# Deferring a layer norm's deviation to the q,k,v eviction, with three reorderings around it, in a fused attention and SwiGLU block

## The chip, the cores and the metric

The kernel runs on one core of one Trainium2 chip, in one launch. The metric is the device time of the run in microseconds; the median over three runs stands for a kernel, and lower is better. A profiled execution is one more run, taken with the hardware profiler; its span is the time from the first to the last instruction.

Engines are named as in the profile: PE (TensorE, matmuls and transposes; PEld its weight loads), DVE (VectorE), ACT (ScalarE), POOL (GpSimd) and SP (SyncE). All DMAs of this kernel are issued on SP's queue. `L333` means line 333 of the kernel in question; in the profile of before these are lines of the kernel before.

## What is computed

A pre-norm transformer block on one sequence of 2048 rows of 640 numbers, all in fp32. The norms have no learned scale or shift.

```python
def _layernorm(x, eps=1e-5):
    m = jnp.mean(x, axis=-1, keepdims=True)
    v = jnp.var(x, axis=-1, keepdims=True)
    return (x - m) / jnp.sqrt(v + eps)

qkv = _layernorm(x) @ wqkv              # 640 -> 3 x 640, 32 heads of 20
# each row attends to itself and to the 7 rows at distances 2, 4, ..., 14 before it
logits = einsum("bhsd,bhswd->bhsw", q, kg) * 20 ** -0.5     # masked where the row does not exist
o = einsum("bhsw,bhswd->bhsd", softmax(logits), vg)
h = x + o @ wo                          # 640 -> 640
n = _layernorm(h)
out = h + (silu(n @ w_gate) * (n @ w_up)) @ w_down          # 640 -> 1728 -> 640
```

## The kernel before

**Blocks.** The 2048 rows are four blocks of 512 (`b` 0 to 3), and each block lies on 128 partitions with four rows per partition (`j` 0 to 3). A row's 640 numbers are five chunks of 128. "Row j" below means such a tile of 128 x 640.

**Precision.** Each fp32 operand of a matmul is split into a high part (rounded by a cast on ACT) and the rest as a low part (a subtraction on DVE). A product is then three matmul passes: high by high, low by high, high by low.

**Stages of a block.**

- First norm (`LnStats` with `ln1`). For blocks 1 to 3 a row takes, on ACT, a pass that sums (L246), the sum times -1/640 (L247) and a pass that sums squares of the centred row (L248). The deviation of all four rows then takes a root on ACT (L258), and on DVE a reciprocal with one Newton step (L259 to L267). A last pass on ACT (L276) subtracts the mean and multiplies by the reciprocal deviation. For block 0, DVE does the statistics (L241, L242) and the last pass (L273), two rows at a time.
- Turning (`to_columns`). PE transposes four 128 x 128 pieces into one PSUM bank (L286), ACT copies the bank to the high part (L289), DVE writes the rest as the low part (L290). A block has five such groups, each of 512 of the 2560 columns of the four rows; so the second group needs rows 0 and 1, the third rows 1 and 2, the fourth rows 2 and 3. Banks 7, 6 and 5 take turns.
- q, k, v (`qkv`). The weights come in four groups `g` of eight heads. For each block, group and row, 15 matmuls of width 480 (L351) go into one of five banks used in turn; this is called a tile below. ACT copies the bank to a staging buffer (L357), and after every second row five DMAs write it to DRAM (L363, L371).
- Attention (`att_load`, `att_qk`, `att_exp`, `att_av`), one block and one group at a time, is done by DVE and a little ACT. K, V and q come back from DRAM (L387, L392); the products of q and K are L400, their sums L405, the softmax L412 to L426, the weighting of V L431 and L439.
- Output projection and second norm (`wo`). The attention output is turned in the same way, PE multiplies by wo (L498, two halves of 320 per row), DVE adds x (L501), and the second norm follows by the same steps as the first (ACT), its result turned again.
- Feed-forward (`ffn`, `finish`). 14 slices of the hidden size: gate and up (L538), silu and product, down (L550) into five banks. At the end DVE adds h (L597, L601) and each row goes out by one DMA (L604).

**Blocks in time.** q, k, v of all blocks come first, in the order block 0, block 1, then blocks 2 and 3 mixed; attention runs on DVE beside them. Block 0's output projection and second norm are put between the last tiles of q, k, v. Then come the four feed-forward stages, each with the next block's output projection inside it.

**What sets the order.** Every step is recorded with an engine, a cost, the ranges it reads and writes, and a priority. `Plan.order` simulates the engines with these costs and fixes the order in which each engine is given its instructions; engines then run strictly in that order. DMAs are costed with an issue time, a shared bus and a latency:

```python
LAT, DV = 3.5, (1.08, 0.05, 1.05, 0.06)
...
            if e == "SP":
                bus = max(bus, end) + nbytes / 320e3
                free[e] = max(free[e], bus - 3.0)
                end = bus + LAT
```

The steps of attention have the lowest priority (20) and yield only to a step of priority 1 that is due soon. In the built program SP's DMAs use eight completion semaphores in turn, so each DMA waits for the one eight before it.

Of the kernel before, what the change touches and what calls it, by code (L numbers as in the profile page):

```python
# [21 lines left out]
GC = D // NG  # L22
# [6 lines left out]
LAT, DV = 3.5, (1.08, 0.05, 1.05, 0.06)  # L29
PR = {'x': 6, 'wqd': 2.5, 'wqh': 0.5, 'wql': 2.5, 'qev': 1, 'kvs': 3, 'atl': 3, 'exp': 8, 'ost': 0.5, 'wod': 6, 'woh': 0.5, 'wol': 2, 'old': 1, 'fld': 3, 'fh': 2, 'fl': 8, 'ln1': 6, 't1': 2, 'wo0': 1.5, 'wo': 2}  # L30


class Plan:
# [23 lines left out]
    def order(self):  # L57
# [15 lines left out]
        while todo:  # L73
# [43 lines left out]
def dve(n):  # L117
    return DV[1] + 0.07 + 0.00104 * n * DV[0]


def tt(n):
    return 0.155 + 0.00104 * n


def act(n):
    return DV[3] + 0.09 + 0.00083 * n * DV[2]


def program(tc, x_in, wqkv_in, wo_in, ffn_in, ffl_in, const_in, out):
# [7 lines left out]
    with tc.tile_pool(name="sb", bufs=1) as sb, tc.tile_pool(  # L137
# [50 lines left out]
        EPSC, BN, MV = LN + 120, LN + 80, LN + 92  # L188
# [39 lines left out]
        class LnStats:  # L228
            def __init__(self, b, src, srcr, prio, on_dve=False):
                self.src, self.srcr, self.prio, self.on_dve = src, srcr, prio, on_dve  # L230
                base = LN + 40 * (b % 2)
                self.SUM, self.NEG, self.SS, self.STD, self.RS, self.TM, self.NB = (base + 4 * i for i in range(7))

            def one(self, j):
                src, xo = self.src, XN + 640 * j
                SUM, NEG, SS = self.SUM + j, self.NEG + j, self.SS + j
                if self.on_dve:
                    def bn():
                        st = f(BN, 12).rearrange("p (a c) -> p a c", c=6)
                        for a in range(2):  # L240
                            V.bn_stats(st[:, a, :], src(j)[:, 320 * a : 320 * a + 320])  # L241
                        V.bn_aggr(f(MV + 2 * j, 2), st)  # L242
                    P.add("DVE", 1.1, bn, r=[self.srcr(j)], w=[rf(BN, 12), rf(MV + 2 * j, 2)], prio=self.prio)
                else:
                    def s1():
                        A.activation(f(xo, 640), src(j), AF.Identity, accum_out=f(SUM, 1))  # L246
                        A.mul(f(NEG, 1), f(SUM, 1), -1.0 / D)  # L247
                        A.activation(f(xo, 640), src(j), AF.Square, bias=f(NEG, 1), accum_out=f(SS, 1))  # L248
                    P.add("ACT", 2.15, s1, r=[self.srcr(j)], w=[rf(xo, 640), rf(SUM, 1), rf(NEG, 1), rf(SS, 1)], prio=self.prio)

            def rstd(self, j, n):
                SS, STD, RS, TM, NEG, NB = (o + j for o in (self.SS, self.STD, self.RS, self.TM, self.NEG, self.NB))
                var, sc, negr = f(SS, n), 1.0 / D, [rf(NEG, n)]
                vr = rf(SS, n)
                if self.on_dve:
                    var = f(MV + 2 * j, 2 * n).rearrange("p (j c) -> p c j", c=2)[:, 1, :]
                    sc, negr, vr = 1.0, [], rf(MV + 2 * j, 2 * n)
                P.add("ACT", 0.2, lambda: A.activation(f(STD, n), var, AF.Sqrt, bias=f(EPSC, 1), scale=sc), r=[vr, rf(EPSC, 1)], w=[rf(STD, n)], prio=self.prio, table="sqrt")  # L258
                P.add("DVE", 0.15, lambda: V.tensor_scalar(f(TM, n), var, sc, EPS, op0=ALU.mult, op1=ALU.add), r=[vr], w=[rf(TM, n)], prio=self.prio)  # L259

                def newton():
                    V.reciprocal(f(RS, n), f(STD, n))
# [3 lines left out]
                    if not self.on_dve:  # L266
                        V.tensor_mul(f(NB, n), f(NEG, n), f(RS, n))  # L267
                P.add("DVE", 1.0, newton, r=negr, w=[rf(STD, n), rf(RS, n), rf(TM, n), rf(NB, n)], prio=self.prio)

            def apply(self, j):  # L270
                xo = XN + 640 * j
                if self.on_dve:
                    P.add("DVE", 0.09 + 0.00052 * 640, lambda: V.tensor_scalar(f(xo, 640), self.src(j), f(MV + 2 * j, 1), f(self.RS + j, 1), op0=ALU.subtract, op1=ALU.mult),  # L273
                          r=[self.srcr(j), rf(MV + 2 * j, 1), rf(self.RS + j, 1)], w=[rf(xo, 640)], prio=self.prio)
                else:
                    P.add("ACT", act(640), lambda: A.activation(f(xo, 640), self.src(j), AF.Identity, bias=f(self.NB + j, 1), scale=f(self.RS + j, 1)),  # L276
                          r=[self.srcr(j), rf(self.NB + j, 1), rf(self.RS + j, 1)], w=[rf(xo, 640)], prio=self.prio)
# [14 lines left out]

        def wq(g, half, k):
            return 4800 * g + 2400 * half + 480 * k
# [6 lines left out]
        def load_x(b, js=range(NJ)):  # L301
            for j in js:
                P.add("SP", 0.55, lambda j=j: Q.dma_start(f(XR + 640 * j, 640), x_in[b, :, j, :]), w=[rf(XR + 640 * j, 640)], prio=0 if b == 0 else PR["x"], nbytes=328e3)

        def ln1(b):
# [3 lines left out]
            st = LnStats(b, src, srcr, 1 if b == 0 else PR["ln1"], on_dve=b == 0)  # L309
# [397 lines left out]
```

## Time and profile before

| | us |
|---|---|
| median of 3 runs (lowest, highest) | 885.89 (885.72, 886.36) |
| profiled execution | 887.53 |
| its span | 885.6 |
| PE busy | 867.5 (98%) |
| DVE busy | 688.7 (78%) |
| ACT busy | 376.7 (43%) |

In the profile, a line of the chain gives start, length and what ran; a line of the timeline adds the instruction's shapes and, in brackets, how long the engine had been idle and what released it; a line of the groups gives the count, the busy time, the mean in ns and the idle time ahead; a line of a table of stretches gives for each engine its busy time and number of instructions (PE, PEld, DVE, ACT, POOL), then PE's granted clock as a share of full speed, the mean share of the 16 DMA engines in use, and GB/s. A line of DMA issues ends with the KB of each and the time from issue to landing.

### The profile page before, as it was taken

How to read it: one execution, taken by the hardware profiler on the slowest of the kernel's cores; microseconds unless marked ns; L12 is line 12 of the kernel's file. 1: busy time of each engine (PE TensorE's matmuls, PEld its weight loads, DVE VectorE, ACT ScalarE, POOL GpSimd, SP SyncE). 2: the span in 40 equal slices, each digit the busy share in tenths (PEclk: the TensorE clock that was granted, in tenths of full speed). 3: DMA queues.
4: the chain of work that ended last, by engine and by line, in shares of the span. 5: the costliest groups of instructions: out<-in, count | busy, mean ns of one | idle time of the engine just before them, and what ended most of it. 6: DMA issues, size and time to landing. Idle time of an engine off the chain costs nothing.

```text
span 885.6 us, 10771 instructions
## 1 busy us (share of the span) xinstructions
PE 867.5 (98%) x4136; PEld 737.8 (83%) x4136; DVE 688.7 (78%) x791; ACT 376.7 (43%) x601; POOL 2.7 (0%) x8
## 2 busy tenths in 40 slices
PE   5999999999999999999999999999999999999998
PEld 4888888898978888888888888888888888888886
DVE  8469999999999999998999999999853336333432
ACT  6757331322375243556243444653433364323321
POOL 0000000000000000000000000000000000000000
PEclk9998999999999999999999999999999999999999
DMA  9894777687656566462755563643243124322201
GB/s 301 244 264 141 193 179 186 156 257 188 166 176 193 149 206 173 142 171 89 232 154 162 184 183 104 177 162 115 90 154 121 53 90 149 120 102 90 90 30 59
DMA packets 64691, 137.17 MB, mean 155 GB/s; under 512 B 6512, under 2 KB 41968, under 8 KB 64640
## 3 DMA queue, kind: packets, MB, share of 16 engines
q1 hardware_dynamic: 64640, 136.49, 51.9%
q8 instruction: 32, 0.52, 0.3%
q14 instruction: 19, 0.16, 0.1%
HBM read 110.18 MB, written 26.29 MB: 154 GB/s over the span
## 4 chain that ended last, share of the span: by engine, by line
PE 93%; DMA 3%; DVE 1%; SPq 1%; ACT 1%; issue 0%; ACTq 0%
PE bank L538 42%; PE bank L550 21%; PE bank L351 20%; PE bank L498 8%; PE bank L286 2%; DMA fa<-in_x_dram 2%; DMA fa<-ksc 1%; DMA fa<-in_wqkv_dram 1%; DVE fa L400 0%; SPq L363 0%; SPq L392 0%; ACT shb L289 0%; PE bank L593 0%; DVE ra L333 0%; SPq L330 0%
## 5 line engine op out<-in xcount | busy, mean ns | idle before, releaser
L538 PE MATMUL bank<-shb,ra 128*128 128x512 f32 x1620 | 381.8, 390 | 1.0 <-ACT shb L289 1.0
L538 PEld LDWEIGHTS bank<-shb,ra 128*128 128x128 f32 x1620 | 302.5, 188 | 63.3 <-ACT shb L289 1.5
L550 PE MATMUL bank<-ra,acts 128*128 128x512 f32 x656 | 163.1, 392 | 0.0
L532 DVE TENSOR_TENSOR ra<-fa,ra 128x640 fp32r<-128x640 f32 (+1 forms) x164 | 131.4, 821 | 24.2 <-ACT ra L522 12.4
L550 PEld LDWEIGHTS bank<-ra,acts 128*128 128x128 f32 x656 | 121.6, 188 | 24.4
L522 ACT CAST ra<-fa 128x1280 fp32r<-128x1280 f32 (+1 forms) x56 | 68.9, 1230 | 125.0 <-PE bank L538 121.0
L351 PE MATMUL bank<-ra,sha 128*128 128x480 f32 x480 | 109.2, 386 | 0.4 <-ACT sha L289 0.3
L570 DVE TENSOR_TENSOR fa<-bank,fa 128x512 f32<-128x512 f32 x52 | 35.8, 689 | 92.5 <-PE bank L538 86.9
L351 PE MATMUL bank<-ra,shb 128*128 128x480 f32 x480 | 105.7, 379 | 0.0
L351 PEld LDWEIGHTS bank<-ra,sha 128*128 128x128 f32 x480 | 91.1, 192 | 15.0 <-ACT sha L289 1.1
L351 PEld LDWEIGHTS bank<-ra,shb 128*128 128x128 f32 x480 | 89.7, 188 | 13.3
L400 DVE TENSOR_TENSOR fa<-fa 128x2560 f32<-128x2560 f32 x32 | 90.3, 2822 | 7.6 <-DMA fa<-ksc 5.3
L431 DVE TENSOR_TENSOR fa<-fa 128x1280 f32<-128x1280 f32 x64 | 93.7, 1487 | 0.7
L439 DVE TENSOR_TENSOR fa<-fa 128x1280 f32<-128x1280 f32 (+2 forms) x96 | 89.7, 934 | 2.4
L405 DVE TENSOR_REDUCE fa<-fa 128x128 f32<-128x2560 f32 x32 | 90.1, 2816 | 0.5
L569 ACT ACTIVATE fa<-bank 128x512 f32<-128x512 f32 x52 | 31.2, 599 | 117.0 <-PE bank L538 116.9
L357 ACT COPY st<-bank 128x480 f32<-128x480 f32 x64 | 35.7, 557 | 100.8 <-PE bank L351 84.3
L498 PE MATMUL bank<-ra 128*128 128x320 f32 x480 | 74.8, 309 | 0.0
L498 PEld LDWEIGHTS bank<-ra 128*128 128x128 f32 x480 | 72.6, 188 | 2.2
L524 ACT CAST ra<-fa 128x640 fp32r<-128x640 f32 x56 | 40.8, 731 | 53.0 <-PE bank L550 52.7
L286 PE MATMUL bank<-fa 128*128 128x128 f32 x240 | 35.7, 286 | 13.1 <-DVE fa L273 8.9
L550 PE MATMUL bank<-acts,ra 128*128 128x512 f32 x164 | 46.4, 391 | 0.0
(64 smaller groups left out, 470.3 us busy)
## 6 DMA issues: line engine op xcount, KB each, us to landing
fa<-in_ffn_dram SPq DMA_DIRECT2D x52, 960.0 KB, 4.7
fa<-ksc SPq DMA_DIRECT2D x32, 440.0 KB, 5.9
fa<-vsc SPq DMA_DIRECT2D x32, 440.0 KB, 5.8
fa<-in_x_dram SPq DMA_DIRECT2D x32, 320.0 KB, 3.3
ksc<-st SPq DMA_DIRECT2D x64, 80.0 KB, 3.7
vsc<-st SPq DMA_DIRECT2D x64, 80.0 KB, 3.0
qsc<-st SPq DMA_DIRECT2D x32, 160.0 KB, 3.0
fa<-qsc SPq DMA_DIRECT2D x16, 320.0 KB, 6.2
```

The source lines that it names most:

```text
L286: T.transpose(banks[bk][:, 128 * q : 128 * q + 128], src(4 * u + q), ident)
L351: T.matmul(banks[bk][:, 0:480], t()[:, o : o + 128], r_(wq(g, w, c), 480), start=p == 0 and c == 0, stop=p == 2 and c == NC - 1)
L400: P.add("DVE", dve(2560), lambda: V.tensor_tensor(f(PROD, 2560).rearrange("p (j w c) -> p j w c", j=2, w=W), window(ko, 2 * jp), f(qo + 32 ...
L405: P.add("DVE", dve(2560), lambda: V.tensor_reduce(f(lo + 128 * jp, 128), f(PROD, 2560).rearrange("p (n d) -> p n d", d=DH), axis=AX.X, op= ...
L431: V.tensor_tensor(f(PROD + 1280 * jj, 1280).rearrange("p (w h d) -> p w h d", w=W, d=DH), f(vo + 160 * j, 1280).rearrange("p (w h d) -> p ...
L439: V.tensor_add(dst(v), v[:, :, 0:m, :], v[:, :, m : 2 * m, :])
L498: T.matmul(banks[bk][:, 0:320], r_(o, 128), r_(m, 320), start=p == 0 and c == 0, stop=p == 2 and c == NC - 1)
L522: P.add("ACT", act(n), lambda: A.copy(r_(gu, n), f(raw, n)), r=[rf(raw, n)], w=[rr(gu, n)], prio=PR["fh"])
L524: P.add("ACT", act(640), lambda: A.copy(r_(dn[0], 640), f(raw + n, 640)), r=[rf(raw + n, 640)], w=[rr(dn[0], 640)], prio=PR["fh"])
L532: P.add(eng, c, lambda o=o: E.tensor_sub(ra[p0:, lo + o : lo + o + 640], fa[p0:, raw + o : raw + o + 640], ra[p0:, hi + o : hi + o + 640]. ...
L538: T.matmul(banks[bk], r_(gu + 1280 * w + wid * c + col, 128), x2(a, c), start=p == 0 and c == 0, stop=p == 2 and c == NC - 1)
L550: T.matmul(banks[k], l, m, start=first and p == 0, stop=last and p == len(passes) - 1)
```

## The change

- **First norm.** It only centres. For rows 0 to 2 of block 0, DVE takes the statistics and subtracts the mean (`one_dve`); for all other rows ACT sums, centres, and takes the squares of the centred row in a step of its own (priority one lower), written over the loaded x. The reciprocal deviations get a place of their own per block (`RS1`), and the q, k, v eviction is an `Identity` activation that multiplies by them. In block 0 they are worked out row by row, elsewhere for four rows at once.
- **Opening.** x rows and the weight loads of the first group alternate one by one; each matmul of block 0's first group is a step of its own that waits for its own chunk; the first weight casts get priority 1.2.
- **Second norm of block 0.** Its deviation is worked out for rows 0 to 2 when row 2 is there, and for row 3 alone. The last q, k, v tile reads the high part of x from a copy (`XH`).
- **Last output row.** Its sum is made in two halves of 256 and written with two DMAs, the second half first.
- **The planner's costs.** DMA latency 1.8 instead of 3.5 us, bus 350 instead of 320 GB/s, issue 0.45 instead of 0.55, larger costs for the small stores, and new costs for ACT and DVE. Priorities `wqh` and `woh` (the other weight casts) go from 0.5 to 3.

The core of the diff, shortened:

```diff
-LAT, DV = 3.5, (1.08, 0.05, 1.05, 0.06)
-PR = {..., 'wqh': 0.5, ..., 'woh': 0.5, ...}
+LAT, RATE = 1.8, 350e3
+PR = {..., 'wqh': 3, ..., 'woh': 3, ...}
...
-                bus = max(bus, end) + nbytes / 320e3
+                bus = max(bus, end) + nbytes / RATE
...
                 def s1():
                     A.activation(f(xo, 640), src(j), AF.Identity, accum_out=f(SUM, 1))
                     A.mul(f(NEG, 1), f(SUM, 1), -1.0 / D)
+                    if self.center:
+                        A.activation(f(xo, 640), src(j), AF.Identity, bias=f(NEG, 1))
+                    else:
                         A.activation(f(xo, 640), src(j), AF.Square, bias=f(NEG, 1), accum_out=f(SS, 1))
...
+                if self.center:
+                    P.add("ACT", 1.0, lambda: A.activation(src(j), f(xo, 640), AF.Square, accum_out=f(SS, 1)),
+                          r=[rf(xo, 640)], w=[self.srcr(j), rf(SS, 1)], prio=self.prio + 1)
...
+            def one_dve(self, j):
...
+                    V.bn_aggr(f(MV + 2 * j, 2), st)
+                    V.tensor_scalar(f(xo, 640), self.src(j), f(MV + 2 * j, 1), None, op0=ALU.subtract)
...
 def ln1(b):
-            if b == 0:
-                for j in range(NJ):
-                    st.one(j)
-                    if j % 2:
-                        st.rstd(j - 1, 2)
-                        st.apply(j - 1)
-                        st.apply(j)
-            else:
-                for j in range(NJ):
-                    st.one(j)
-                st.rstd(0, 4)
-                for j in range(NJ):
-                    st.apply(j)
+            for j in range(NJ):
+                (st.one_dve if b == 0 and j < 3 else st.one)(j)
+            st.prio = 2
+            for j in range(NJ) if b == 0 else ():
+                st.rstd(j, 1)
+            if b:
+                st.rstd(0, NJ)
...
 def qkv(b, g):
+                moved = (b, g, j) == (NB - 1, NG - 1, NJ - 1)
+                if moved:
+                    P.add("ACT", act(640), lambda j=j: A.copy(r_(XH, 640), ...), ..., prio=3)
...
-                for ps in ((0,), (1,), (2,)) if b == g == 0 else ((0, 1, 2),):
+                whole = tuple((p, c) for p in range(3) for c in range(NC))
+                for ps in [(x,) for x in whole] if b == g == 0 else [whole]:
...
-                P.add("ACT", act(480), lambda bk=bk, so=so: A.copy(stage_t()[:, so : so + 480], banks[bk][:, 0:480]), r=[pb(bk)], ...)
+                P.add("ACT", act(480), lambda bk=bk, so=so, j=j: A.activation(stage_t()[:, so : so + 480], banks[bk][:, 0:480], AF.Identity, scale=f(RS1 + 4 * b + j, 1)),
+                      r=[pb(bk), rf(RS1 + 4 * b + j, 1)], ...)
...
 def wo(b, prio, bks):
                 stats.one(j)
-            return stats
+                if j == NJ - 1 or (j == 2 and prio < PR["wo"]):
+                    lo, n = (0, NJ) if prio >= PR["wo"] else ((0, 3), (3, 1))[j - 2]
+                    stats.rstd(lo, n)
+                    for q in range(lo, lo + n):
+                        stats.apply(q)
...
 def finish(b):
+                cuts = (0, 256, 512) if b == NB - 1 and j == NJ - 1 else (0, 512)
+                pieces = list(zip(cuts, cuts[1:]))[::-1]
+                for o, e in pieces:
...
-        load_x(0, (0, 1))
+        load_x(0, (0,))
         P.add("SP", ..., Q.dma_start(f(MASK, 160), const_in), ...)
-        load_wqkv(0, (0, 1, 2))
+        load_wqkv(0, (0, 1))
+        load_x(0, (1,))
+        load_wqkv(0, (2, 3))
         load_x(0, (2,))
-        load_wqkv(0, (3, 4))
+        load_wqkv(0, (4,))
         load_x(0, (3,))
```

More of the change, by code (lines that the diff above doesn't have):

```diff
@@ L251, in rstd, with s1 @@
-            def rstd(self, j, n):
[L252 to L259, printed above, removed]
+                def s1():
+                    A.activation(f(xo, 640), src(j), AF.Identity, accum_out=f(SUM, 1))
+                    A.mul(f(NEG, 1), f(SUM, 1), -1.0 / D)
+                    if self.center:
+                        A.activation(f(xo, 640), src(j), AF.Identity, bias=f(NEG, 1))
+                    else:
+                        A.activation(f(xo, 640), src(j), AF.Square, bias=f(NEG, 1), accum_out=f(SS, 1))
@@ new lines, in qkv, with mm @@
+                if moved:
+                    P.add("ACT", act(640), lambda j=j: A.copy(r_(XH, 640), t()[:, 640 * j : 640 * j + 640].bitcast(F32)), r=[(nm, 640 * j, 640 * j + 640)], w=[rr(XH, 640)], prio=3)
+                def mm(ps, j=j, bk=bk, moved=moved):
+                    for p, c in ps:
+                        a, w = passes[p]
+                        o = 2560 * a + 640 * j + 128 * c
+                        l = r_(XH + 128 * c, 128) if moved and a == 0 else t()[:, o : o + 128]
+                        T.matmul(banks[bk][:, 0:480], l, r_(wq(g, w, c), 480),
+                                 start=p == 0 and c == 0, stop=p == 2 and c == NC - 1)
```

129 lines of the change are left out of this document (61 added, 68 removed).

## Prediction, made before the changed kernel ran

> **What bounds the kernel now.** First the head of the page: who is busy, and through whom the chain runs that ends last.
>
> ```profile
> span 885.6 us, 10771 instructions
> PE 867.5 (98%) x4136; PEld 737.8 (83%) x4136; DVE 688.7 (78%) x791; ACT 376.7 (43%) x601; POOL 2.7 (0%) x8
> PE 93%; DMA 3%; DVE 1%; SPq 1%; ACT 1%; issue 0%; ACTq 0%
> ```
>
> PE sets the end. The change leaves its matmuls and transposes as they are (the same counts line by line), so it can only give or take time in which PE waits or runs slowly. Where that is, the chain in order of time tells (start, length, what; pieces left out between them):
>
> ```profile
> 16.91 16.92 PE bank L351 x76
> ...
> 40.96 9.32 DMA fa<-in_x_dram
> 50.30 6.84 DMA fa<-in_x_dram
> 57.16 6.55 DMA fa<-ksc
> 63.73 2.83 DVE fa L400
> 67.54 0.93 ACT fa L276
> 68.51 2.82 PE bank L286 x12
> 71.33 4.55 PE bank L351 x15
> 96.21 1.31 PE bank L286 x12
> 97.52 25.94 PE bank L351 x120
> 258.73 14.15 PE bank L538 x60
> 878.40 3.47 PE bank L550 x15
> ```
>
> Undisturbed, a q,k,v matmul takes 25.94 / 120 = 0.216 us (a tile of 15: 3.24) and a transpose 1.31 / 12 = 0.109. PE is off this pace in four places: before 16.91; around 68.5; just ahead of 258.73; and after 881.9, where only the last output is left. Then what PE waited for, and its clock (column PEclk, the third from the right):
>
> ```profile
> PE bank L286 <- DVE fa L273: 8.9, 2, 8.5
> PE bank L286 <- ACT fa L276: 3.3, 1, 3.3
> 67.00:68.00 1.00, 0.00 (x0) 0.00 (x0) 0.93 (x4) 0.46 (x1) 0.00 (x0) 0.62 0.35 88
> 68.00:74.00 6.00, 5.49 (x20) 5.00 (x21) 5.93 (x8) 4.80 (x8) 0.00 (x0) 0.50 0.87 262
> 39.00:58.00 19.00, 19.00 (x94) 16.56 (x93) 14.71 (x11) 10.45 (x26) 0.00 (x0) 1.00 1.01 269
> fa<-ksc SPq DMA_DIRECT2D x32, 440.0 KB, 5.9
> ```
>
> The wait before 68.51 is 3.3 us, and PE then ran on half its clock: 12 transposes in 2.82 instead of 1.31, 15 matmuls in 4.55 instead of 3.24. The place costs 3.3 + 1.5 + 1.3 = 6.1 us. Its cause is the chain above: attention's second K load was issued at 57.16, behind the x loads, and landed at 63.7; DVE stood at the product of L400 in front of block 2's deviation (four Newton steps), and the norm's last step (L276) and PE's transposes waited for that.
>
> **The change, part by part.** *Opening.* Rows used:
>
> ```profile
> 3.73 0.89 DVE L241 BATCH_NORM_STATS2 fa<-fa 128x6 f32<-128x320 f32 x2 [1.66 <-DMA fa<-in_x_dram]
> 7.85 1.14 DVE L273 TENSOR_SCALAR fa<-fa 128x640 f32<-128x640 f32 x2
> 4.97 0.43 SPq L303 DMA_DIRECT2D fa<-in_x_dram  x1
> fa<-in_x_dram SPq DMA_DIRECT2D x1, 320.0 KB, 6.1
> 4.02 5.63 DMA fa<-in_wqkv_dram
> 13.42 0.16 DVE L263 TENSOR_TENSOR fa<-fa 128x2 f32<-128x2 f32 x1
> 13.62 0.16 DVE L264 SCALAR_TENSOR_TENSOR fa<-fa 128x2 f32<-128x2 f32 x1
> 14.95 0.75 ACT L246 ACTIVATE fa<-fa 128x640 f32<-128x640 f32 x1 [0.24 <-DMA fa<-in_x_dram]
> 16.04 0.83 ACT L248 ACTIVATE fa<-fa 128x640 f32<-128x640 f32 x1
> L289 ACT CAST sha<-bank 128x512 fp32r<-128x512 f32 x10 | 5.4, 589 | 0.0
> L290 DVE TENSOR_TENSOR sha<-bank,sha 128x512 fp32r<-128x512 f32 x10 | 6.4, 684 | 0.9 <-ACT sha L289 0.8
> L333 DVE TENSOR_TENSOR ra<-fa,ra 128x480 fp32r<-128x480 f32 x20 | 12.0, 652 | 2.7 <-ACT ra L331 2.7
> ```
>
> I measure by an equivalent start: the moment from which PE, at full pace, would have done the same. Before, 15 tiles and 40 transposes are done when PE stops at 68.51 - 3.32 = 65.19: 65.19 - 225 x 0.216 - 40 x 0.109 = 12.2. After: the first eight loads are the same bytes in another order, so x2 lands where the eighth landed, 4.02 + 5.63 = 9.65, and x3 at 4.97 + 6.1 = 11.1. By bytes between 3.73 and 9.65, x1 lands near 6.8. One row on DVE is statistics 0.89, their aggregate about 0.25 and a subtraction 1.14 / 2: 1.7. DVE has two weight residuals (L333, 0.65 each) first and ends x1 at 9.1, then a residual copy (0.68), then x2 at 11.6. ACT casts the fifth weight, copies x's second group, and centres x3 from 11.5 for 16.04 + 0.83 - 14.95 = 1.9: 13.4. The last two groups of transposes (8 x 0.109) end at 14.3, with 11 matmuls done among them: 14.3 - 20 x 0.109 - 11 x 0.216 = 9.7 as equivalent start. I add 0.7 for a clock still low (PE is sparsely busy until 11.5, and the next two copies of 0.59 come behind x3's square) and 0.3 for waits on single copies: 10.7, a **gain of 1.5**. Ends: 2.2 with neither, 0 if PE stays slow for 4 us more. The deviations move behind this: 4 rows x 5 steps x 0.2 (13.62 - 13.42) are 4 us on DVE instead of two groups; they delay the last two low weight parts: on DVE 11.6 + copy 0.7 + 10 steps 2.0 + copy 0.7 + weight 0.65 + two copies 1.4 + 10 steps 2.0 + two weights 1.3 = 20.4. PE asks for the last at its 41st matmul, 10.7 + 2.2 + 40 x 0.216 = 21.5: hidden, with 1 us to spare. The eviction's multiplication waits for a deviation now; a bank is asked for again only five tiles (13 us of PE) later, so 64 such evictions cost nothing. Should that cover go, PE waits for Newton steps, as before.
>
> *The middle.* Transposes of blocks 1 to 3 need centring alone, so Newton steps no longer stand before them. But the program asks for them earlier: block 2's first group after tile 11 instead of 15, the second and third after tile 12, the fourth after 14. From the equivalent start, tile 11 ends at 10.7 + 11 x 3.24 + 40 x 0.109 = 50.7, and tile 14 at 50.7 + 12 x 0.109 + 3 x 3.24 = 61.7. Block 1 first: its first centring stands on ACT behind six weight casts, 13.4 + three copies 1.8 + square 1.0 + two roots 0.6 + casts 3.5 + 1.9 = 22.2, and PE asks for it two matmuls into tile 4, at 10.7 + 2.2 + 47 x 0.216 = 23.1: hidden if those weights land in time. SP waits, at each DMA, for the one eight before it, so loads queue. x2's first row is issued at 40.9 as before (the row 40.96), but one K half and Q went out before the stores; 1.35 MB of K and V plus its own 0.33 at 269 GB/s (the row 39:58) is 6.2 us: lands 46 to 47.5, centred by 49.5. Needed at 50.7: hidden. The next two rows are issued as soon as the V halves land (45, 46) and follow on ACT at 1.9 each with an eviction and a square between, to about 51.5 and 54; needed at 54.4 and 54.7: hidden, by 0.7 for the second.
>
> The second K is the hard point. In the new order DVE does the product with it **before** the residual copy of block 2's first group, for which PE's fourth group waits (same bank). From the first K's second half (39.1) to this one 5.2 MB go out (five K or V halves of 440 KB, four x rows, one of wo, one of q, two sets of stores): 19.3 us, so 58.4. Product 2.83, copy 0.68: 61.9, against 61.7. I take 1.5 us for all waits of this stretch together (0 to 3.3), none over 2 us, so no clock drop: **gain 6.1 - 1.5 = 4.6**.
>
> *Second norm of block 0.* Rows:
>
> ```profile
> 241.97 0.88 DVE L501 TENSOR_TENSOR h<-bank,fa 128x320 f32<-128x320 f32 x2
> 249.30 1.74 ACT L276 ACTIVATE fa<-h,fa 128x640 f32<-128x640 f32 x2 [0.86 <-DVE fa L267]
> 254.18 1.47 PE L286 MATMUL bank<-fa 128*128 128x128 f32 x12
> ```
>
> Before, all 20 transposes come after the last q,k,v tile, 254.2 to 258.73: 4.55 us for 2.18 of work, 2.35 lost to copies. After, rows 0 to 2 are normalised at once and row 3 alone, and tiles stand between the groups: the last two groups go ahead of the last tile, whose 3.24 us cover two copies (1.2). Before, the way from row 3's addition to the end of the last L276 was 241.97 to at least 249.30 + 4 x 0.87 = 252.8, 11 us with four rows in it; row 3 alone needs about three L276 less, 8 to 9, where the new order leaves four tiles, 13 us. An extra table load and a copy of 640 on ACT sit in the same slack. **Gain 1.9**, ends 0 and 2.35 (0.4 for the last residual copies, which the third pass of the first FFN tile asks for).
>
> *Last output row.*
>
> ```profile
> 879.32 3.62 SPq L604 DMA_DIRECT2D out_dram<-h  x4
> 881.89 0.69 DVE L597 TENSOR_TENSOR h<-bank,h 128x512 f32<-128x512 f32 x1 [0.44 <-PE bank L550]
> out_dram<-h SPq DMA_DIRECT2D x1, 320.0 KB, 2.2
> ```
>
> One addition of 0.69 and one DMA of 320 KB become two additions, about 0.13 longer together, and two DMAs, the first some 0.3 earlier, the last only 128 KB. The data thus start 0.3 earlier. **Gain 0.3**, ends -0.2 (a second issue on SP) and 0.6.
>
> Sum: 1.5 + 4.6 + 1.9 + 0.3 = 8.3. The profiled execution took 887.53, 1.93 beyond its span, and becomes 879.2; the median of the runs is 885.89, 1.64 below it, and becomes **877.6**.
>
> **The clock, row and rule.** PE stopped at 65.19; with a mean of 0.62 between 67 and 68 the clock halved at 67.24, 2.05 us into the wait, and held until 74. So I price any new wait over 2 us at 2.8 more. [...]
>
> **The rivals.** *The wait moves with its clock drop*: K lands near 61 instead of 58.4, PE waits 61 + 3.5 - 61.7 = 2.8, and 2.8 more by the clock: the middle gains 0.5 instead of 4.6, **881.7**. For it: DMA share 1.01 in this stretch, and my slack is below 1 us. Chance 0.15.
>
> *DVE gives it back*: attention on DVE sets when block 0's output projection can run, so what PE gains before is lost there; only norm and tail stay, 885.89 - 2.2 = **883.7**. For it: DVE is 78% busy over all. Against: the new order asks three tiles later, and DVE's own longest wait (K at 63.7) shrinks too. 0.06.
>
> *The order does not deliver*: no gain in the opening (tile 14 then ends at 63.2), and K at 65, little later than the 63.7 of before: product and copy to 68.5, PE waits 5.3 + 2.8 = 8.1 instead of 6.1; with 2.2 from norm and tail **885.7**. 0.08.
>
> *Slower*: the second K, at its new place in front of the copy, lands later than before, because SP waits for stores that lie behind the x loads. From 67.0 on PE loses 8.8 + 2.8, 1.8 us more than all gains return; at 67.5 it is 9.3 + 2.8 = 12.1 against 6.1, less 3.7 of gains: **888.2**. Against: the same traffic landed it at 63.7. 0.11.
>
> **How the numbers follow.** 0.60 is left for the forecast, whose own range is 874.7 (all upper ends: 11.2) to 880. 0.2% (1.8 us) is about what a measurement can tell: 884.1 and 887.7. Faster: 0.60 + 0.14 + 0.05 = 0.79; same: 0.08 and the 0.02 left of the second and third case, 0.10; slower 0.11. The range goes from 874.7 to 884.8 and leaves out the last two rivals.
>
> **What would show it.** Right: PE's equivalent start near 10.7; no idle over 2 us and PEclk 1.00 between 17 and 254; the first FFN matmul within 0.5 us of the last q,k,v tile; 2.7 us or less from PE's end to the span's end. Wrong: PEclk below 1 after 20 us, a PE wait on DVE's residual copy or ACT's centring near 23, 50, 62 or 72 us (block 3), or any new wait of over 1 us in the FFN, where I expect none.

## The result and the profile after

| | us |
|---|---|
| before, median of 15 runs (lowest, highest) | 885.72 (884.41, 887.92) |
| after, median of 15 runs (lowest, highest) | 889.66 (886.12, 895.22) |
| after / before | 1.0043, 95% interval 1.0026 to 1.0061 |
| profiled execution of after, its span | 895.22, 893.4 |

The change makes the kernel 0.43% slower; 877.6 was predicted. The runs of after also spread wider (9.1 us from lowest to highest against 3.5), and the profiled execution is the slowest of the 15: what it shows lost is 5.6 us more than a typical run loses, and its single waits are to be read with that in mind. Part of the spread is PE's clock: the runs with a mean granted clock of 1.000 took 886.7 to 889.2, those with 0.996 or 0.997 took 891.0 to 895.2.

The head of the page of after:

```profile
span 893.4 us, 10812 instructions
PE 869.9 (97%) x4136; PEld 738.4 (83%) x4136; DVE 687.0 (77%) x801; ACT 388.4 (43%) x613; POOL 2.7 (0%) x8
```

PE still sets the end. What it waited for in after (line, releaser, then us in total, times, longest):

```profile
PE bank L298 <- DVE sha L302: 4.2, 1, 4.2
PE bank L298 <- ACT fa L247: 4.0, 2, 3.2
PE bank L362 <- ACT sha L301: 2.4, 2, 1.8
PE bank L298 <- DMA fa<-osc: 2.2, 2, 1.6
PE bank L298 <- DVE ra L302: 0.8, 1, 0.8
PE bank L567 <- DVE acts L597: 0.7, 1, 0.7
```

(`sha`, `shb` and `ra` hold the split operands of matmuls, `osc` is the attention output in DRAM, `acts` the products of silu.) The one wait of 3.3 us of before has become 8.2 us in three: centring (L247) for block 2's transposes, and the residual copy (L302) that holds the fourth group's bank. The waits for the output projection's input are new too: near 205 us for a residual (0.8, output `ra`), near 210 for the attention output (1.6), and 0.6 once more in the FFN. The chain of after shows what is behind the first of them:

```profile
36.77 8.14 DMA fa<-ksc
44.92 3.95 DMA fa<-vsc
...
54.49 6.22 DMA fa<-in_wo_dram
60.73 8.32 DMA fa<-ksc
...
71.82 0.69 DVE sha L302
...
72.56 1.11 PE bank L298 x4
73.67 8.64 PE bank L362 x30
...
262.04 3.25 PE bank L362 x15
265.29 13.60 PE bank L555 x60
```

The second half of the second K is issued at 60.73 and lands at 69.05, where the prediction had 58.4. Its product (2.82) and the copy (0.69) follow, PE starts again at 72.56, and for the next 9.8 us it does four transposes and 30 matmuls that take 6.9 at full pace. At the end of the extract the first FFN matmul follows the last q,k,v tile without a gap. The stretches around the wait (PE's busy time is the first column after the length, its clock the third from the right):

```profile
40.00:57.00 17.00, 13.83 (x71) 11.79 (x70) 10.58 (x12) 8.96 (x21) 0.00 (x0) 1.00 1.02 272
67.00:72.00 5.00, 1.37 (x7) 0.87 (x5) 2.93 (x2) 3.06 (x6) 0.00 (x0) 0.94 0.98 217
72.00:77.00 5.00, 4.45 (x13) 3.89 (x14) 4.90 (x9) 1.86 (x4) 0.00 (x0) 0.50 0.98 307
```

Why the data are late shows in SP's timeline (start, length, what was issued). First before, then after:

```profile
23.69 0.53 SPq L330 DMA_DIRECT2D fa<-in_wqkv_dram  x1
26.91 2.86 SPq L456 DMA_DIRECT2D fa<-in_wo_dram  x4
37.65 1.42 SPq L392 DMA_DIRECT2D fa<-ksc  x2
```

```profile
30.43 0.54 SPq L338 DMA_DIRECT2D fa<-in_wqkv_dram  x1
34.83 1.88 SPq L469 DMA_DIRECT2D fa<-in_wo_dram  x4
36.77 0.51 SPq L405 DMA_DIRECT2D fa<-ksc  x1
42.82 0.49 SPq L405 DMA_DIRECT2D fa<-ksc  x1
46.41 0.52 SPq L317 DMA_DIRECT2D fa<-in_x_dram  x1
```

The last weight load of q,k,v goes out 6.7 us later, four loads of wo (1.3 MB) stand right ahead of the first K instead of 10 us earlier, and the first K's second half waits at SP for the eighth DMA before it, the fourth of those wo loads: 42.8 instead of 38.4. Block 2's first x row goes out at 46.41, not 40.96, and ACT begins on it at 54.03.

### The profile page after: what moved, and what is told of

Read it like the earlier page. It is cut to its first block, busy times and chain, and to the rows that moved or that the text cites. A ratio compares the mean times of both kernels' runs of the same rounds, so it can differ in the third digit from the quotient of the medians.

```text
span 893.4 us, 10812 instructions
## 1 busy us (share of the span) xinstructions
PE 869.9 (97%) x4136; PEld 738.4 (83%) x4136; DVE 687.0 (77%) x801; ACT 388.4 (43%) x613; POOL 2.7 (0%) x8
## 4 chain that ended last, share of the span: by engine, by line
PE 91%; DMA 5%; DVE 2%; ACT 1%; SPq 1%; issue 1%; DVEq 0%; ACTq 0%
PE bank L555 40%; PE bank L362 20%; PE bank L567 20%; PE bank L511 8%; PE bank L298 3%; DMA fa<-ksc 2%; DMA fa<-osc 1%; DMA fa<-in_wo_dram 1%; DVE fa L413 1%; DMA fa<-in_wqkv_dram 1%; DMA fa<-vsc 0%; ACT ra L339 0%; DVE fa L418 0%; SPq L376 0%; DVE ra L549 0%
## 5 line engine op out<-in xcount | busy, mean ns | idle before, releaser
L362 PE MATMUL bank<-ra,sha 128*128 128x480 f32 x480 | 112.4, 392 | 2.4 <-ACT sha L301 2.4
L362 PEld LDWEIGHTS bank<-ra,shb 128*128 128x128 f32 x470 | 87.6, 188 | 12.8
L369 ACT ACTIVATE st<-bank,fa 128x480 f32<-128x480 f32 x64 | 42.0, 660 | 94.7 <-PE bank L362 78.0
L298 PEld LDWEIGHTS bank<-fa 128*128 128x128 f32 x240 | 30.5, 147 | 24.6 <-DVE fa L264 5.4
```

What stands on the lines that cost most here:

```text
L298: T.transpose(banks[bk][:, 128 * q : 128 * q + 128], src(4 * u + q), ident)
L362: T.matmul(banks[bk][:, 0:480], l, r_(wq(g, w, c), 480), start=p == 0 and c == 0, stop=p == 2 and c == NC - 1)
L369: P.add("ACT", act(480), lambda bk=bk, so=so, j=j: A.activation(stage_t()[:, so : so + 480], banks[bk][:, 0:480], AF.Identity, scale=f(RS1 ...
```

## The experiments

Runs of one group were timed beside the kernel before on one chip: before took 885.78 beside e1 to e5, 885.56 beside e6 to e9, 884.40 beside e10 to e13. So medians of different groups compare through the ratios. Four kernels move single steps within one engine's list and leave every other list as after has it; the lists are then merged again by their dependencies. `low` is a weight chunk's low part (group, chunk), `newton` a deviation of block 0 (row), `turn` a group of four transposes, `rest` its residual copy (6 to 10 block 1, 11 to 15 block 2, 16 to 20 block 3, 21 to 25 block 0's output projection), `qk` a product with K (block, group, half), `mm` a tile (block, group, row).

```diff
+        seq = {e: [n for n in P.order() if P.ops[n][0] == e] for e in ("PE", "ACT", "DVE", "POOL", "SP")}
+        move([...], before)      # within one engine's list
```

| run | kernel | median | ratio to before, 95% interval |
|---|---|---|---|
| e1 | after, low parts first on DVE | 889.26 | 1.0044 (1.0027 to 1.0060) |
| e2 | after, one residual copy first on DVE | 890.27 | 1.0051 (1.0032 to 1.0069) |
| e4 | after, PE's transposes of blocks 2 and 3 later | 888.53 | 1.0032 (1.0017 to 1.0047) |
| e5 | all of these | 888.53 | 1.0038 (1.0023 to 1.0054) |
| e6 | after, two DMA figures of the planner | 883.40 | 0.9967 (0.9955 to 0.9979) |
| e7 | after, all planner figures of before | 899.69 | 1.0150 (1.0136 to 1.0163) |
| e8 | before, planner figures of after | 891.74 | 1.0070 (1.0058 to 1.0082) |
| e9 | after, filled opening | 886.73 | 1.0013 (0.9999 to 1.0027) |
| e10 | before, second norm in two steps | 885.33 | 1.0002 (0.9991 to 1.0014) |
| e11 | before, deferral alone | 891.38 | 1.0068 (1.0052 to 1.0084) |
| e12 | before, figures as in e6 | 883.10 | 0.9984 (0.9975 to 0.9992) |
| e13 | e6, filled opening | 881.51 | 0.9961 (0.9948 to 0.9975) |

### One wait at a time: e1, e2, e4, e5

**e1.**

```diff
+        move([("low", 0, 3), ("low", 0, 4)], ("rest", 4))
+        move([("newton", 2), ("newton", 3)], ("low", 2, 0))
```

> The kernel after with only DVE's order changed in the first 25 us: the low parts of the first group's last two weight chunks and those of the second group stand ahead of block 0's last deviations (Newton steps of rows 2 and 3). Theory A, late data: those Newton steps held weight slots that SP wanted to load into (SP waited 4.5 us in one piece), the DMA engines ran at 150 GB/s from 16 to 24 us, and so everything behind came late. Then SP's longest wait for the residuals of L341 falls from 4.5 to under 2 us, x's first row of block 2 and the second half of the second K land 3 to 4 us earlier (54.0 and 69.1 in the profile of after), and the waits for centring (3.2 and 0.9 us) go; the wait for the residual of block 2's first group stays at about 4, because PE now asks earlier too; median about 886.5. Rival B or C (DVE's or PE's own order at block 2 is the cause, or landings are set by the stores and the eight outstanding DMAs): K still lands at 68 to 69, time within 1 us of the 889.7 of after.

SP's waits for the residuals of L341 before 40 us, first of after, then of e1, and PE's waits in e1:

```profile
SPq L338 <- DVE ra L341: 7.4, 9, 4.5
```

```profile
SPq L338 <- DVE ra L341: 4.0, 9, 1.5
```

```profile
PE bank L298 <- ACT fa L247: 2.7, 2, 1.9
PE bank L298 <- DVE sha L302: 2.7, 1, 2.7
```

The mechanism is there: SP's longest wait falls from 4.5 to 1.5 us, ACT begins block 2's first row at 51.6 instead of 54.0, the product with the second K starts at 65.2 instead of 69.1. The time does not follow: 889.26. From 20 us on SP ran into the next thing in its list, the stores of the first tiles, which wait for evictions near 24 us. Theory A explains part of the lateness and none of the median.

**e2.**

```diff
+        move([("rest", 11)], ("qk", 0, 1, 0))
```

> The kernel after with one instruction moved on DVE: the residual copy of block 2's first group ahead of the product with the second K. Theory B, DVE's order: the wait of 4.2 us goes, and the half clock behind it, 4 to 7 us of the profiled execution; the next residuals, which stand behind the sums and the weighting of V, then hold the fifth group and block 3's groups for some 2 us; median about 886.5. Theory C (PE's transposes of block 2 stand too early in its queue, whatever DVE does first): the wait moves to the next groups with its clock drop, median 888 to 890. Theory A alone (only the landing of the data counts): as C.

The wait of 4.2 us is gone, as theory B says. In its place PE waits 1.6 us at 79 for the next residual, the waits for centring (2.3) and osc stay, and 890.27 is what theory C expected.

**e4.**

```diff
+        move([("turn", 11)], ("mm", 0, 3, 1)); move([("turn", 12)], ("mm", 0, 3, 2))
+        move([("turn", 13)], ("mm", 0, 3, 3)); move([("turn", 14)], ("mm", 1, 0, 0))
+        move([("turn", 15)], ("mm", 1, 0, 1))
+        move([("turn", 16), ("turn", 17), ("turn", 18)], ("mm", 1, 1, 0))
```

> The kernel after with only PE's order changed: block 2's five groups of transposes each one or two tiles later, block 3's first three behind the fourth tile of block 1 instead of the first. Their columns are wanted only from the 33rd tile on. Theory C: with the data as late as before (K at about 69) the waits of 3.2, 0.9 and 4.2 us and the half clock fall to about 2 us together; worked out from the median of before: 885.7 + 0.6 (opening) - 6.1 (its stall in the middle) - 2.35 + 2.35 (second norm, and the waits for the attention output near 205) + 1.3 (FFN) + 2 = 883.5. Theories A and B, with DVE and DMA as the bound: the waits come back a few tiles later, median 887 or more.

The stretches of e4, and its longest wait:

```profile
40.00:87.00 47.00, 46.83 (x236) 40.32 (x236) 35.93 (x39) 37.12 (x83) 0.00 (x0) 1.00 0.85 226
87.00:186.00 99.00, 94.36 (x433) 81.66 (x432) 97.07 (x85) 26.73 (x44) 0.00 (x0) 0.97 0.70 178
```

```profile
PE bank L298 <- DVE shb L302: 4.6, 1, 4.6
```

Between 40 and 87 us PE now waits 0.17 us in all, with full clock. But at 121 us it stops for 4.6 us: block 3's transposes need a residual copy that stands on DVE behind attention's next products, and DVE (97.07 us busy of 99) gets there no earlier.

**e5** adds the output projection's transposes to all three:

```diff
+        move([("turn", 24)], ("mm", 2, 3, 0)); move([("turn", 25)], ("mm", 2, 3, 2))
```

> The three edits of the other runs together, and the last two groups of block 0's output projection one and two tiles later (they waited 0.8 and 1.6 us near 205 and 210 for a residual and for the attention output). Theory C with A and B as contributions: no wait of PE over 1 us between 20 and 265 us, clock full; by the same sum 885.7 + 0.6 - 6.1 - 2.35 + 1.3 = 879.1. Rival, DVE gives it back: what PE gains before 190 it waits for at the attention output near 205, 883 to 885.

Missed by 9 us: the same 4.6 us near 122, then small waits near 205 to 250. In the four kernels a wait went or shrank when its cause was taken away; the first FFN matmul came at about 260 us in e1, e4 and e5 alike, and the median stayed at 888.5 to 890.3. So the loss has no single place: the list as a whole is out of step.

### Why the list is out of step: e6, e7, e8, e12

The planner of the kernel gives each step a time while it makes the list, and the step that ends an attention unit (its store of the output, L445 or L458) can be set against the chip. These are the planner's own numbers, no measurement; beside them the issue of that store in the trace:

| kernel | plan: first unit, end of all | chip: first unit, median |
|---|---|---|
| before | 86.4, 891.0 | 88.0, 885.7 |
| after | 79.8, 881.1 | 95.1, 889.7 |
| e8 | 82.1, 886.2 | 87.1, 891.7 |
| e6 | 85.7, 887.0 | 84.9, 883.4 |
| e7 | 96.9, 903.2 | 98.5, 899.7 |
| e10 | 86.4, 890.5 | 84.5, 885.3 |
| e11 | 97.1, 897.7 | 96.6, 891.4 |
| e12 | 91.3, 891.1 | 85.7, 883.1 |

With the change's DMA figures (after, e8) the chip is 5 to 15 us behind the plan at the first unit and 5.5 to 8.6 us above it at the end; with the other figures it is within 6 us and 3.5 to 8 us below. The change's latency of 1.8 us and 350 GB/s stand against median landings of 3 to 8 us, kind by kind, between 30 and 75 us and 270 to 275 GB/s in the full stretches (272 in the row 40:57). The opening is another matter: there after moved 352 GB/s (5.4 to 17.3 us), so 350 fits the first microseconds and not the middle.

One profile tells the time of the first unit only roughly: e10 has the plan of before up to there, and its unit ended at 84.5 against 88.0. The 15 us of after also come from the slowest of its runs; e9, which has the lists of after and only fills PE's waits in the opening, ended that unit at 88.4, still 8.6 behind its plan.

**e6.**

```diff
-LAT, RATE = 1.8, 350e3
+LAT, RATE = 3.5, 280e3
```

> The kernel after with two figures of the planner changed: DMA latency 3.5 us instead of 1.8 and bus 280 GB/s instead of 350 (the timeline shows 270 to 275 where the DMA engines are full). Theory P: in the order of after the plan ends block 0's attention units at 79.8, 105.9, 134.1, 160.8 us, the chip at 95.1, 121.6, 149.1, 176.0, while the plan of before (86.4, 113.4, 142.8, 170.5) is met within 2 us (88.0, 115.6, 143.5, 171.8); so after places what PE needs from DVE and from DMAs 10 to 15 us too early in PE's queue. With these figures the plan says 85.7, 111.5, 140.3, 166.9: the waits of PE between 40 and 215 us fall from 11 to below 5 us and the median to 883 to 885. Rival E (the edits themselves, the deferral above all, cost the time): the median stays at 888 to 890.

```profile
40.00:186.00 146.00, 146.00 (x707) 127.18 (x706) 136.79 (x126) 68.28 (x131) 0.00 (x0) 1.00 0.77 210
```

```profile
252.14 14.18 PE L555 MATMUL bank<-shb,ra 128*128 128x512 f32 x60 [0.35 <-ACT shb L301]
```

Right, at 883.40. With one line changed and every other edit of the change in place, PE does not wait once from 40 to 186 us, the second K's product starts at 61.6 without waiting for the DMA, and the first FFN matmul comes at 252.14 (before: 258.73, after: 265.29).

**e7** takes all figures and the two priorities back (gathered and shortened here).

```diff
-LAT, RATE = 1.8, 350e3
+LAT, RATE = 3.5, 320e3
-'wqh': 3, ... 'woh': 3, nbytes=130e3, nbytes=250e3, issue 0.45, dve(n) = 0.155 + 0.00104 * n, act(n) = 0.155 + 0.00087 * n
+'wqh': 0.5, ... 'woh': 0.5, nbytes=82e3, nbytes=164e3, issue 0.55, dve(n) = 0.12 + 0.00112 * n, act(n) = 0.15 + 0.00087 * n
```

> The kernel after with all planner figures and the two priorities of before: the edits to the norms, the opening and the last row alone. Theory P: no slower than before, 883 to 886, if the order that comes out does not put attention late (its plan ends the first unit at 96.9, later than before). Rival E: 888 to 890, as after.

Missed: 899.69, the slowest of all. Here the plan and the chip agree (first unit 96.9 and 98.5): the list itself is bad, with attention 10 us later than before, and the second norms of later blocks wait for it (6.9 us at one in the FFN). The planner takes the next ready step by priority and looks no further, so another set of steps can send it down a worse path that its own total of 903.2 shows.

**e8** is before with `LAT, RATE = 1.8, 350e3`, the priorities and the step costs of after, and nothing else.

> The kernel before with the planner figures and the two priorities of after and none of the other edits. Theory P: its plan ends the first attention units at 82.1, 107.5, 135.6, 162.8; the chip will end them 5 to 10 us later, PE gets new waits, and the median rises to 887 to 890. Rival E: within 1 us of before, 885.7.

```profile
PE bank L285 <- ACT fa L275: 4.6, 2, 3.2
PE bank L285 <- DMA fa<-osc: 2.6, 3, 1.8
```

891.74: without any edit to the norms, the opening or the last row, the new figures alone cost 6.2 us, and leave the same marks as in after, PE stopped at block 2's transposes and at the output projection's input.

**e12** is e8 with `LAT, RATE = 3.5, 280e3`.

> The kernel before with the planner figures and priorities of after, but DMA latency 3.5 us and bus 280 GB/s, and none of the other edits: what the figures that made the edits faster than before are worth without them. Theory P with edits that are worth something: its plan ends at 891.1, with such figures the chip came out 3.6 below, so about 887; the edits then bring 3 to 4 of the difference to the 883.4 with them. Rival, the gain came from the figures alone: 883 to 884.

883.10. In ratios to their own runs of before, 0.9984 here and 0.9967 in e6: the figures bring about 0.16%, the edits about as much again, and that second part is no larger than what the two intervals leave open. The rival was nearer than the forecast.

### The parts alone: e10, e11

**e10.**

```diff
+                if prio < PR["wo"] and j >= 2:
+                    stats.rstd(0 if j == 2 else 3, 3 if j == 2 else 1)
...
+                    P.add("ACT", act(640), lambda j=j: A.copy(r_(XH, 640), ...), ...)
```

> The kernel before with one part of the change: block 0's second norm in two steps (rows 0 to 2, row 3) and the copy of x's high part that the last q,k,v tile reads. The order up to 200 us is that of before. If the gap of 2.35 us ahead of the first FFN matmul was worth what the prediction took for it: no gap of over 0.5 us there, median 883.9. Rival, the FFN gives it back (DVE is 95% busy there and the planner's end falls by only 0.5, from 891.0 to 890.5): the gap goes, and 885.0 to 885.7 remains.

PE's waits from 230 us on:

```profile
PE bank L357 <- ACT ra L350: 0.9, 1, 0.9
PE bank L548 <- ACT shb L289: 0.8, 1, 0.8
PE bank L286 <- DVE fa L588: 0.4, 1, 0.4
```

The gap of 2.35 us is gone. 0.9 of it comes back as a wait for the copy of x (L350), and the last two, 1.2 us together, stand near 413, at the next block's second norm, where before had none. Ratio 1.0002: the rival was right.

**e11.**

```diff
-                for j in range(NJ):
-                    st.apply(j)          # blocks 1 to 3: centring only, deviation to RS1
...
+  A.activation(..., AF.Identity, scale=f(RS1 + 4 * b + j, 1)) if b else A.copy(...)
```

> The kernel before with the deferral alone, in blocks 1 to 3 (block 0's norm, the opening, the second norm, the last row and the planner as before). If the deferral by itself is worth the stall at block 2 that it was to remove: 880 to 882. Theory P (the order that the planner makes of it decides): its plan ends block 0's attention units at 97.1, 123.4, 152.5, 179.7 against 86.4, 113.4, 142.8, 170.5 and the whole at 897.7 against 891.0; with the old figures the chip came out 3.5 to 5.4 below the plan, so 892.3 to 894.2.

891.38, a little below the forecast of theory P. PE's waits from 265 us on:

```profile
PE bank L300 <- ACT fa L290: 4.7, 2, 4.1
```

The first FFN matmul came at 253.8, 4.9 us earlier than before, and all of it and more was lost behind it: attention ran 8 to 9 us late from its first unit (96.6), and PE waited for the second norms of later blocks, 4.7 us near 578; the mean clock from 500 to 700 us is 0.97, which makes some 12 us of half clock (0.03 x 200 / 0.5, an estimate, the mean being given to 0.01).

### The opening: e9, e13

```diff
+        for t, n in (("w1", 8), ("w2", 5), ("w3", 6), ("w4", 5)):   # e9: 8, 4 and 1
+            P.add("PE", 0.0, lambda: [T.matmul(banks[4][:, 0:128], f(PROD, 128), f(PROD + 128, 128), ...) for _ in range(n)], ...)
```

> The kernel after with 13 small products of zeros into an unused bank, which keep PE busy where it waits before 12 us (8 ahead of the first transposes, 4 behind them, 1 behind the second group). In the profile of after the matmuls ran at half pace until 17.0 us, in that of before until about 13; the equivalent start was 12.8 against 12.2. Theory W: a trickle of work does not raise the clock, a filled one does: with the filling the pace is full from about 9 us on and the equivalent start is 10.5 to 11.3. As the waits behind it hang on data and on DVE, the median falls by 0 to 1 us only, to about 889. Rival: data hold the opening, the equivalent start stays at 12.5 to 13.

PE's timeline of before, of after and of e9 (a matmul of q,k,v takes 0.216 us at full pace, a transpose 0.109; a line is some 0.2 longer than these add up to, as with 1.31 for ten transposes):

```profile
14.68 1.31 PE L286 MATMUL bank<-fa 128*128 128x128 f32 x10 [0.38 <-DVE fa L273]
```

```profile
5.44 1.11 PE L298 MATMUL bank<-fa 128*128 128x128 f32 x4 [5.44 <-DVE fa L264]
13.65 2.35 PE L362 MATMUL bank<-ra,sha 128*128 128x480 f32 x5
17.07 8.05 PE L362 MATMUL bank<-ra,sha 128*128 128x480 f32 x36
...
56.01 0.66 PE L298 MATMUL bank<-fa 128*128 128x128 f32 x4 [3.17 <-ACT fa L247]
```

```profile
5.47 0.66 PE L303 MATMUL bank<-fa 128*128 128x128 f32 x4
11.48 0.91 PE L367 MATMUL bank<-ra,sha 128*128 128x480 f32 x2 [0.74 <-ACT sha L306]
15.93 8.04 PE L367 MATMUL bank<-ra,sha 128*128 128x480 f32 x36
```

In before the transposes at 14.68 run at full pace; in after the five matmuls at 13.65 still take 0.47 each. Filled from 2.12 us on (e9), the transposes at 5.47 run at full pace, but behind the remaining waits (1.1 and 0.7 us) half pace is back: the four transposes at 12.19 take 1.05 and the five matmuls at 12.90 take 2.35, and the mean clock from 8.50 to 17.32 is 0.81. The equivalent start is 16.17 - 11 x 0.216 - 20 x 0.109 = 11.6 against 12.8: a partial filling. The median gains 2.9 us, more than the 0 to 1 forecast. In its profile the three waits of the middle are 2.2, 0.9 and 1.9 us at full clock, against 3.2, 0.9 and 4.2 with half clock in the slowest run of after; whether the other 1.7 come from there is not settled.

> The kernel after with latency 3.5 us and 280 GB/s in the planner, and 24 small products of zeros that fill PE's waits before 12 us. With the figures alone the equivalent start was 12.3 and PE had no wait over 1 us from 20 to 500 us, so here an earlier opening should arrive at the end: equivalent start 10.3 to 11.3, median 881.8 to 882.4. Rival, what is gained early is waited for later at DVE or a DMA: 883.0 to 883.4.

```profile
56.61 1.04 PE L302 MATMUL bank<-fa 128*128 128x128 f32 x8
250.06 14.14 PE L559 MATMUL bank<-shb,ra 128*128 128x512 f32 x60 [0.35 <-ACT shb L305]
```

With the waits filled all the way, 13 tiles and 40 transposes are done at 56.61: equivalent start 56.61 - 195 x 0.216 - 4.36 = 10.1, 2.1 us ahead of e6, which stands at the same point at 58.67. The trace keeps this to the end: the first FFN matmul comes at 250.06 against 252.14, the span is 879.7 against 881.8. The median, 881.51, lies just under the range and 1.9 below that of e6, but e6 ran on another chip, and the ratios (0.9961 and 0.9967) differ by less than their intervals; so the 2 us are seen in one trace of each and not shown by the medians. The kernel is 0.39% (0.25 to 0.52) faster than before, the lowest ratio here, and by the ratios 0.8% faster than after.

## Why the prediction was wrong, point by point

The sum was to move the span by -8.3 us; the profiled spans moved by +7.8. Of the 16.1 between them the points below name 15; 1 us of small waits is not assigned. The medians moved by +3.9, so some 4 us of this belong to the profiled run and not to a typical one.

- **Opening: +1.5 forecast, -0.6 measured.** PE stopped at 52.84 (56.01 - 3.17) with 11 tiles and 40 transposes done: equivalent start 52.84 - 165 x 0.216 - 4.36 = 12.8, against 12.2 before and 10.7 forecast. The data came about as worked out (x1 centred at 9.9, x2 at 12.1, x3 at 13.8; forecast 9.1, 11.6, 13.4). Mis-sized was the allowance of 0.7 for a low clock: the trickle of single matmuls left PE at half pace until 17. The end given for that case was 0, and it fell below even that. e13 bears out the other terms: with the waits filled it started at 10.1, where the sum without the clock's 0.7 gives 9.7 + 0.3 = 10.0.
- **Middle: +4.6 forecast, about -5 measured** (8.2 of waits and 2.8 of half pace against 6.1). The step that failed is the count "From the first K's second half (39.1) to this one 5.2 MB go out ...: 19.3 us, so 58.4", in its start and in its bytes. 39.1 is the moment at which the issue of that half ended in before; like "x2's first row is issued at 40.9 as before", it was carried over from the order of before. In after that issue ended at 43.3 (42.82 + 0.49), 4.2 us later, and from there to the landing at 69.05 are 25.7 us instead of 19.3. The stretch of after:

```profile
42.80:69.05 26.25, 21.53 (x105) 17.98 (x103) 14.62 (x14) 18.81 (x44) 0.00 (x0) 1.00 0.97 254
```

254 GB/s for 26.25 us are 6.7 MB, 1.5 more than counted: the count took the bus as free at its start, while the first half of that K, issued at 36.77, landed only at 44.9. In before, too, that stretch had taken 24.6 us (39.1 to 63.7). The centring of block 2's first row, forecast for 49.5 and called hidden, ended at 55.95. I had worked out that the deviations delay the low weight parts and hidden that behind PE alone; the weight slots they free are also what SP loads into, and SP's list stands still behind them (7.4 us of such waits in after before 40 us, 4.0 in before).
- **"DVE gives it back", 0.06.** In the form given, PE's gain lost at the output projection, it did not happen in after, since there was no gain. But e4 and e5 show a kin of it as soon as the middle is mended: a copy that stands behind attention's products on DVE holds PE for 4.6 us, earlier than this rival had it. In e6 DVE is nearly as busy (136.8 us of 146) and PE does not wait, so the order decides, not DVE's load alone.
- **The slower rival, 0.11,** named the mechanism at 67: a K that lands late because of what stands before it on SP. It was right in kind, at 69.05, and its price (8.8 + 2.8 from 67.0 on) counts the one wait; PE's own lateness of 4 us by then, through centring that the prediction called hidden, made that wait shorter and the sum about the same.
- **Second norm: +1.9 forecast, 2.35 measured at its place**, no gap ahead of the first FFN matmul. It went again: 2.35 us of new waits (osc and residual) around 205 and 210, and 1.26 in the FFN, where 624.4 us lie between the first matmul and PE's end against 623.1. "Any new wait of over 1 us in the FFN, where I expect none" was nearly right in size (0.6 and 0.7) and wrong as a sum. e10 shows that the part alone is worth nothing.
- **Last row: +0.3 forecast, 0.0 measured.** From PE's end to the span's end 3.73 us before and 3.74 after: the issue of the last DMA ends 0.24 later after PE's end, and what follows it is as much shorter. The sign named for this part, 2.7 us or less, did not follow from the sum: 3.73 - 0.3 is 3.4.
- **The clock's price.** Forecast: 2.8 more for any wait over 2 us. Measured: 3.17 us in after cost nothing more (clock 1.00 throughout), 2.30 in e2 and 2.71 in e1 came with half clock for 3.4 us, 4.18 in after and 4.64 in e4 for 6.8, 4.62 in e5 for 3.4 again. So the length of a wait alone, 2 us or another, did not set the price here; the last section has the rows.
- **What no step had: the planner.** The prediction counted each edit against the trace and took the list as given. e6, e8 and e12 show that the two DMA figures, which carry no instruction, moved the time by 6 to 8 us (1.0043 to 0.9967 and 1.0070 to 0.9984 of before), more than the other edits bring under the same figures (0.9984 to 0.9967). Under the figures of before those edits even cost 1.5% (e7), again through the list that came out. The list of after was there to be read, and its distances (x issued, K issued, transposes wanted) were read against the times of before. Open is which of the two figures matters more, whether values between these two pairs would do as well, and why e12 lies so far below its plan.

## What to carry to other kernels

Where an order is made from modelled costs, set a few of the model's own times beside the trace before any edit is priced: here one line of DMA figures moved the time by 0.8%, and all the changes to the computation, under the better figures, by about 0.2%. A wait that is mended by itself in a list that is out of step comes back at the next place where two engines meet; e1, e2, e4 and e5 took such waits away and gained 1.1 us at most. And a moment taken from the old trace holds for the new order only if everything ahead of it on the same queue is still ahead of it.

## What the runs showed of the hardware

- The half clock that came with a wait of PE lasted 3.41 us in e1, e2 and e5, and 6.8 in before, after and e4. Half-microsecond stretches (PE's busy time, then its clock) of e2 and of after, at the fall and at the rise:

```profile
55.50:56.00 0.50, 0.29 (x2) 0.62 1.13 359
59.00:59.50 0.50, 0.50 (x4) 0.97 0.75 110
```

```profile
71.00:71.50 0.50, 0.00 (x0) 0.90 1.04 247
78.00:78.50 0.50, 0.50 (x4) 0.78 0.59 165
```

With 0.50 in between, e2's half clock lasts from 55.62 to 59.03, 3.41 us, and that of after from 71.40 to 78.22, 6.82. By the same reading it was 6.83 in before and in e4, 3.41 in e1 and e5. The length of the wait does not tell which: 2.30 us (e2), 2.71 (e1) and 4.62 (e5) go with 3.41, and 3.32 (before), 4.18 (after) and 4.64 (e4) with the longer ones. The wait of 3.17 us in after, from 52.84 to 56.01, costs nothing more: the clock from 52 to 57 is 1.00, and the four transposes behind it take 0.66. What decides between these cases was not shown.
- Matmul work in pieces, with waits of 0.7 to 1.8 us between them, did not raise PE's pace for over 10 us (after: four transposes at 5.44 took 1.11 us, the five matmuls at 13.65 still 2.35, the eight transposes at 15.79 1.52; at 17.07 the 36 matmuls took 8.05, full pace). Filled without a break from 2.12, PE was at full pace at 5.47 (e9, four transposes in 0.66). In these first microseconds the clock in the rows reads 1.00 all the same (after, from 5 to 10 and from 10 to 16); so the half pace is to be read from the durations.
- With the DMA engines nearly full, a load of 440 KB took 8.1 us from issue to landing (at 36.77, share 1.02 meanwhile) and 8.3 (at 60.73, 0.86), and one x row of 320 KB 7.6 (at 46.41, 1.01), against 6.1 for the fourth x row in the opening of before (1.00). The share went with no fixed rate: in these four stretches the engines moved 294, 224, 240 and 340 GB/s.
- The eviction that multiplies by a deviation (128 x 480) took 0.66 us on ACT where the plain copy took 0.56; it was hidden, as forecast.
